# Tile 3's sums on VectorE and GpSimd placed anew, one preparation later, and another order of matmuls in the retention blocks

## The chip, the cores and the metric

One core of a Trainium2 chip. The time is that of the device for one execution of the whole program, in microseconds (us). TensorE (PE) multiplies matrices; its weight loads (PEld) run beside its matmuls. VectorE (DVE), ScalarE (ACT) and GpSimd (POOL) work elementwise, SyncE (SP) issues most of the transfers. Each engine runs its own instructions in order; semaphores hold an instruction back until another engine's result is there.

## The reference

A retention layer (attention with decay instead of a softmax) feeds a two-layer network whose activation is `h * cos(h)`:

```
B, H, S, D = 8, 8, 576, 64
ret = (q @ k.T) / sqrt(D) * Dmat     # Dmat[i, j] = gamma_h ** (i - j) if i >= j, else 0
x   = (ret @ v), heads side by side  # 4608 tokens x 512
h   = x @ w_in                       # 512 -> 2048
g   = h * cos(h)
out = g @ w_out                      # 2048 -> 512
```

All inputs and the output are float32; the kernel multiplies in bfloat16 and adds up in float32.

## The kernel before

The 4608 tokens are 36 groups of 128. The network takes them in ten tiles, of 512, 256 and 256 tokens and then seven of 512. Tile 3 is the first of these seven (in the code `S7 = 3`) and holds groups 8 to 11; tile 4 holds groups 12 to 15.

**Retention.** A group is loaded (`load`, three transfers for q, k and v on SyncE's queue into five buffers each), prepared on GpSimd (`prep`: q and k times powers of gamma, lines 139 and 140, and v cast to bfloat16, line 147), and transposed by a transfer on SyncE's queue (`transposes`, line 156). SyncE takes loads, transposes and stores in the order in which the code asks for them, and a transpose waits there until GpSimd has prepared its group. `scores` multiplies key by query on TensorE and masks the result to `ret` on VectorE (line 192). `states` keeps the running sum of key times value (TensorE line 242, VectorE lines 263 and 265; ScalarE copies it to `sb`, line 256). `attn_out` gives the group's result out of two kinds of matmul into one PSUM bank: state times query (line 283) and `ret` times v (line 296); ScalarE copies it to `xT`. From tile 3 on, `unit7` does this for two groups at a time: `states` for the next, `attn_out` for these two, and then the scores of the two after them. These are the retention blocks; PSUM bank "b" serves the states first and the second of the two scores afterwards.

**Network.** `mm1` makes `h` in eight blocks of a tile (line 323); ScalarE takes the cosine (line 331), VectorE multiplies both to `gT` (line 332). From tile 3 on the second matmul goes by Winograd's form of Strassen's method: the tile is cut into 2 x 2 quarters, and seven products of quarters replace eight. They run in the order 3, 4, 5, 2, 1, 7, 6 (`mm2_seven`, `product`, line 455). Products 3 and 4 read `gT` itself, the others a sum or difference of two quarters of `gT`, called X5, X2, X1, X7 and X6 here, in two halves of 128x1024 each (`g_sum`, line 401). `on_dve` there says which sums go to VectorE; all others go to GpSimd, and the first GpSimd sum after a VectorE sum is made to wait for it ("port free"). `sums_after` places the sums behind the blocks of `mm1`; tile 3 has placings of its own, there and in `more_sums`. In tile 3 these blocks go through the first half of the tokens (blocks 0 to 3) and then the second half (4 to 7); X5 needs the first half alone.

In tiles 3 and 4 the retention work stands inside the seven products like this: before product 5 only scores (`scores2`), before product 1 a retention block, before product 6 another, in tile 3 without scores. Tile 3 computes the scores of groups 12 to 15, tile 4 those of 16 to 21.

**What is prepared when.** Each store of a quarter of the output calls `feed`, which prepares groups up to a count that the code sets, then asks for their transposes and for further loads. Before tile 3, 16 groups (0 to 15) are prepared. During tile 3 the counts after its four stores are 17, 18, 19 and 22; in tile 4 they are 22, 23, 24 and 26. Group 16 is prepared by `more_sums`, so that the first of these calls finds it done. The order on each engine is the order of the code: nothing is scheduled anew.

Of the kernel before, what the change touches and what calls it, by code (L numbers as in the profile page):

```python
# [17 lines left out]
def kernel(  # L18
# [16 lines left out]
    nc = tc.nc  # L35
    P = 128
    B, H, S, D = q.shape
    assert (B, H, S, D) == (8, 8, 576, 64)
    HG = H // 2
# [4 lines left out]
    NG = NTOK // P  # L44
    PER = 2 * S // P
    MIX = PER // 2
    HP = P // 2
# [7 lines left out]
    starts = [sum(widths[:n]) for n in range(len(widths))]  # L55
    N_PE_T = 6
    S7 = 3
# [42 lines left out]
    tiles = {}  # L100
# [167 lines left out]

        return add

    def attn_out(gs, bank, evac=nc.vector.tensor_copy):


        ps = psum.tile([P, len(gs), HG, P], F32, tag=bank, name="ov")
        for x, g in enumerate(gs):
            c = g % PER
            if c == 0:
                continue
            qT = tiles["a", g][3]
            sb = tiles.pop(("sb", g))  # L280
            n = HP if c == MIX else P
            for hg in range(HG):
                nc.tensor.matmul(  # L283
                    ps[:, x, hg, :n],
                    lhsT=sb[:, hg, :],
                    rhs=qT[:, hg, :n],
                    start=(hg == 0),
                    stop=False,
                    skip_group_check=True,
                )  # L290
        for x, g in enumerate(gs):
            vb = tiles["a", g][1]
            ret = tiles.pop(("ret", g))
            for hg in range(HG):
                for he in range(2):
                    nc.tensor.matmul(  # L296
                        ps[he * D : he * D + D, x, hg, :],
                        lhsT=vb[:, 2 * hg + he, :],
                        rhs=ret[:, he, hg, :],
                        start=(g % PER == 0 and hg == 0),  # L300
                        stop=(hg == HG - 1),
                        skip_group_check=True,
                    )
        n = max(m for m in range(len(starts)) if starts[m] <= gs[0] * P)
        if ("x", n) not in tiles:
            tiles["x", n] = xp.tile([P, DG, 512], BF16, tag="xT", name="xT")
        t0 = gs[0] * P - starts[n]
        evac(  # L308
            tiles["x", n][:, :, t0 : t0 + len(gs) * P].rearrange("p c (x i) -> p x c i", i=P), ps
        )  # L310
# [43 lines left out]
    E2 = ET // 2  # L354
    N2 = DM // 2
    w_sum = {}
    last = len(widths) - 1
# [25 lines left out]
    def g_sum(n, x, e0, e1):  # L383

        gT = tiles["g", n]
        a, b, op_ = {
            5: ((0, 0), (0, 1), ALU.add),
            2: ((1, 0), (1, 1), ALU.add),
            1: ((0, 0), (1, 1), ALU.add),
            7: ((0, 1), (1, 1), ALU.subtract),  # L390
            6: ((1, 0), (0, 0), ALU.subtract),
        }[x]
        if ("gs", n, x) not in tiles:
            tiles["gs", n, x] = sump.tile([P, E2, 256], BF16, tag=f"gs{x}", name=f"gs{x}")
        i0, i1 = (
            gT[:, k * E2 + e0 : k * E2 + e1, r * 256 : (r + 1) * 256] for r, k in (a, b)
        )
        on_dve = x == 5 or (n, x) in ((S7, 1), (S7, 2)) or (n, x, e0) in (
            (last, 1, 0), (last, 2, 4), (S7 + 1, 2, 4)
        )  # L400
        i = (nc.vector if on_dve else nc.gpsimd).tensor_tensor(  # L401
            out=tiles["gs", n, x][:, e0:e1], in0=i0, in1=i1, op=op_
        )
        if on_dve:
            tiles["gate"] = i
        elif "gate" in tiles:
            tc.add_manual_dep(
                i.ins,
                tiles.pop("gate").ins.name,
                mybir.DependencyInfo(mybir.DependencyClass.Sync, mybir.DependencyReason.DATA),  # L410
                reason="port free",
            )

    def sums_after(n, i):

        if n == S7:
            if i < 4:
                w_sums(3 + i % 2, i // 2 * 4, i // 2 * 4 + 4)
            if i == 6:
                g_sum(n, 5, 0, 4)  # L420
            elif i == 7:
                g_sum(n, 5, 4, E2)
                g_sum(n, 2, 0, E2)
                g_sum(n, 7, 0, 4)
        elif i in (3, 7):
            for x in (5, 2, 1, 7, 6) if n < last or i > 3 else (5, 1, 2, 7, 6):
                g_sum(n, x, i - 3, i + 1)

    def product(n, x):
# [31 lines left out]
                skip_group_check=True,  # L461
            )
        return parts

    def more_sums(n):

        if n == S7:
            g_sum(n, 7, 4, E2)
            prep_next()
            g_sum(n, 1, 0, E2)  # L470
            for e in (0, 4):
                g_sum(n, 6, e, e + 4)

    def mm2_seven(n, at):

# [63 lines left out]
    def prep_next():  # L539
        nonlocal prepared  # L540
        prep(prepared)
        prepared += 1

    def feed(s):

        nonlocal loaded, prepared, transposed
        before = loaded
        n, r = divmod(s - starts[S7] // P, 4)
        if n >= 0:
            while prepared < min(NG, starts[S7] // P + 10 + 4 * n + ((0, 1, 2, 4) if n else (-1, 0, 1, 4))[r]):  # L550
                prep_next()
            while transposed < prepared:
                transposes(transposed)
                transposed += 1
            ahead = starts[S7] // P + 14 if n == 0 and r < 3 else prepared + LD
            while loaded < min(NG, prepared + LD, ahead):
                load(loaded)
                loaded += 1
            return
        while True:  # L560
            while prepared < min(loaded, 2 * s + 7, s + 11, starts[S7] // P + 8):
                prep(prepared)
                prepared += 1
                if transposed < N_PE_T:
                    transposed += 1

            if N_PE_T <= transposed < min(prepared, s + 11) and (
                transposed <= loaded - 2 or loaded == NG or (s > 3 and loaded == before)
            ):
                transposes(transposed)  # L570
                transposed += 1
            elif loaded < min(NG, 2 * s + 8, s + 13):
                load(loaded)
                loaded += 1
            else:
                break
# [58 lines left out]
    for h0, bank, evac in ((0, "b", nc.scalar.copy), (HG, "m", nc.vector.tensor_copy)):  # L635
# [8 lines left out]
        ps = psum.tile([P, 2, P, G4], F32, tag=bank, name="tr")  # L644
        for r in range(G4):
            for j in range(2):
                nc.tensor.matmul(
                    ps[:, j, :, r],
                    lhsT=qs4[:, r, h0 + 2 * j : h0 + 2 * j + 2, :].rearrange("p h d -> p (h d)"),
                    rhs=ident,  # L650
                    start=True,
                    stop=True,
# [42 lines left out]
    def scores2(g):  # L695
        if g < NG:
            scores(g, "a")
            scores(g + 1, "b")
# [12 lines left out]
    def unit7(g, more=True, then=lambda: None):  # L711

        copy = states([g + 1, g + 2], "b")()
        then()
        attn_out([g, g + 1], "m", nc.scalar.copy)
        if more:
            scores2(g + 2)
        copy(nc.scalar.copy)

    late = []  # L720
    for n, w in enumerate(widths):
# [8 lines left out]
        else:  # L730
            m = 1024 // w
# [17 lines left out]
        g = starts[n] // P + w // P  # L749
        if n == 0:  # L750
            todo = [
                (34 + 5 * i, lambda x=x, e=e: w_sums(x, e, e + 4))
                for i, (x, e) in enumerate((x, e) for x in (1, 6, 7) for e in (0, 4))
            ] + [
                (45, lambda: transposes(4, "ab")),
                (49, lambda: state(4)),
                (50, lambda: scores(4, "a")),
                (57, lambda: attn_out([4], "a")),
                (61, lambda: transposes(5, "ba")),
                (63, lambda: state(5)),  # L760
            ]
        elif n == 1:
            todo = pair(6, "ab", 16, 27)
        elif n == 2:
            todo = [(11, lambda: scores2(g)), (25, lambda: unit(g, "m", soon=True))]
            late += [lambda: unit(g + 2, "b", False)]
        else:
            at = {}
            if n + 1 < len(widths):
                at = {  # L770
                    5: lambda then: unit7(g, True, then),
                    1: lambda then: unit7(g + 2, True, then),
                }
                if n in (3, 4):
                    at = {
                        5: lambda then: (then(), scores2(g), more_sums(n)),
                        1: lambda then: unit7(g, True, then),
                        6: lambda then: unit7(g + 2, n > 3, then),
                    }
            mm2_seven(n, at)  # L780
            continue
        todo.sort(key=lambda u: u[0])
        order = [(tsi, et) for tsi in range(w // P) for et in range(ET)]
        if n == 0:

            part = 3 * ET // 4
# [38 lines left out]
```

## Time and profile before

| what | value |
|---|---|
| median of three runs | 302.14 us (302.12 to 302.67) |
| the profiled execution | 302.56 us, of which 300.9 us is its span |
| TensorE busy / idle in 94 to 124 us (tile 3 and the start of 4) | 27.74 / 2.26 us |
| TensorE busy / idle in 124 to 151 us (rest of tile 4) | 24.69 / 2.31 us |
| TensorE busy / idle in 151.2 to 181.4 us (tile 5) | 30.09 / 0.11 us |
| GpSimd busy in the same three | 25.71, 25.68, 25.00 us |

The granted TensorE clock is 1.00 throughout. "Idle" is the stretch less the busy time. Lines of the profile such as `98.80 0.60 POOL L147 CAST vb<-fv ... x1` give the start and the length in us, the engine, the line of the kernel, the operation, the tile written and those read, and how many instructions were merged; in brackets stands the idle time before and what ended it.

### The profile page before, as it was taken

What the parts mean: (1) busy time and instruction counts of PE and PEld (TensorE: products, weight loads), DVE (VectorE), ACT (ScalarE), POOL (GpSimd) and SP (SyncE); (2) the same over time, 40 slices, a digit from 0 to 9 for tenths busy, and PEclk for the clock granted to TensorE, in tenths of its full rate; (3) what the DMA queues carried; (4) which work ended last, traced back from release to release, by engine and by line L of the source; (5) the groups of instructions that cost most, each with busy time, mean ns of one, the idle gap of its engine ahead of it and who ended that gap; (6) DMA issues with size and microseconds to landing.
All of it is one profiled execution on the core that took longest, in us unless ns stands there. A gap on an engine that the chain in (4) does not pass through costs nothing.

```text
span 300.9 us, 6641 instructions
## 1 busy us (share of the span) xinstructions
PE 288.5 (96%) x2740; PEld 199.4 (66%) x2761; DVE 209.7 (70%) x250; ACT 145.7 (48%) x187; POOL 200.2 (67%) x165
## 2 busy tenths in 40 slices
PE   7899999999999979997999999999999999999995
PEld 3478647858588867465844885488448854884594
DVE  6777636664699994789858774877488748835872
ACT  3556333515255354651456574648465646524620
POOL 2770076445445499999975997599859925970583
PEclk9999999999999999999999999999999999999999
DMA  8999999999999999999999988994850250022013
GB/s 210 212 210 207 206 219 191 207 253 199 219 184 201 204 215 226 225 258 188 193 247 216 243 212 147 236 215 122 184 131 2 72 139 2 0 72 70 2 35 105
DMA packets 154269, 50.23 MB, mean 167 GB/s; under 512 B 140800, under 2 KB 153216, under 8 KB 154240
## 3 DMA queue, kind: packets, MB, share of 16 engines
q1 hardware_dynamic: 150016, 45.63, 75.1%
q0 software_dynamic: 4224, 4.19, 8.4%
q8 instruction: 21, 0.34, 0.5%
q14 instruction: 8, 0.07, 0.1%
HBM read 36.70 MB, written 9.44 MB: 153 GB/s over the span
## 4 chain that ended last, share of the span: by engine, by line
PE 51%; DVE 1%; issue 0%; DVEq 0%
PE h L323 23%; PE o L455 22%; PE ov L296 2%; PE sc L183 2%; PE ov L283 2%; PE st L242 1%; DVE ret L192 1%; DVE ot L484 0%; DVEq L820 0%
## 5 line engine op out<-in xcount | busy, mean ns | idle before, releaser
L401 POOL TENSOR_TENSOR gs<-gT 128x1024 bf16<-128x1024 bf16 x49 | 104.9, 2173 | 43.0 <-DVE gs L401 42.4
L323 PE MATMUL h<-xT,w_in_sb 128*128 128x512 bf16 (+2 forms) x820 | 127.1, 313 | 1.4 <-DVE gT L332 0.5
L332 DVE TENSOR_TENSOR gT<-h,cosh 128x1024 bf16<-128x1024 f32 x72 | 87.9, 1223 | 43.6 <-ACT cosh L331 43.4
L331 ACT ACTIVATE cosh<-h,half_pi 128x1024 f32<-128x1024 f32 x72 | 80.2, 1114 | 64.1 <-PE h L323 62.9
L323 PEld LDWEIGHTS <-w_in_sb 128*128 128x128 bf16 x832 | 75.8, 98 | 49.8 <-issue 1.1
L139 POOL TENSOR_TENSOR qks<-fq,gq 128x512 bf16<-128x512 f32 x32 | 35.5, 1109 | 38.7 <-DMA fq<-in_q_dram 36.7
L455 PEld LDWEIGHTS <-gs 128*128 128x128 bf16 x576 | 53.9, 98 | 9.4 <-issue 1.9
L140 POOL TENSOR_TENSOR qks<-fk,gk 128x512 bf16<-128x512 f32 x35 | 37.4, 1068 | 9.8 <-DMA fk<-in_k_dram 9.1
L192 DVE TENSOR_TENSOR ret<-sc,tri 128x1024 bf16<-128x1024 f32 x32 | 38.0, 1219 | 3.8 <-PE sc L183 3.7
L455 PE MATMUL o<-ws,gs 128*128 128x256 bf16 (+1 forms) x352 | 38.4, 268 | 0.0
L484 DVE TENSOR_TENSOR ot<-o,ot 128x512 f32<-128x512 f32 (+2 forms) x32 | 19.7, 620 | 14.7 <-PE o L455 14.6
L340 PE MATMUL o<-w_out_sb,gT 128*128 128x512 bf16 x121 | 28.8, 380 | 0.4 <-issue 0.2
L308 ACT CAST xT<-ov 128x1024 bf16<-128x1024 f32 (+1 forms) x18 | 16.5, 918 | 25.8 <-PE ov L296 25.6
L455 PE MATMUL o<-w_out_sb,gs 128*128 128x256 bf16 x224 | 25.8, 273 | 1.8 <-DVE ot L484 1.8
L455 PE MATMUL o<-w_out_sb,gT 128*128 128x256 bf16 x224 | 25.6, 273 | 0.0
L455 PEld LDWEIGHTS <-gT 128*128 128x128 bf16 x224 | 21.8, 98 | 3.9
L340 PEld LDWEIGHTS <-gT 128*128 128x128 bf16 x128 | 11.8, 98 | 12.6
L401 DVE TENSOR_TENSOR gs<-gT 128x1024 bf16<-128x1024 bf16 (+1 forms) x19 | 19.6, 1046 | 0.4
L256 ACT CAST sb<-s 64x256 bf16<-64x256 f32 x40 | 16.1, 403 | 0.9 <-DVE s L263 0.4
L147 POOL CAST vb<-fv 128x512 bf16<-128x512 f32 x22 | 13.9, 632 | 2.6 <-DMA fv<-in_v_dram 2.4
L350 ACT COPY ot<-o 128x512 f32<-128x512 f32 x8 | 4.7, 588 | 17.1 <-PE o L340 17.0
L484 DVE TENSOR_TENSOR ot<-ot,o 128x512 f32<-128x512 f32 x14 | 9.6, 682 | 4.7 <-ACT ot L509 2.7
(70 smaller groups left out, 174.2 us busy)
## 6 DMA issues: line engine op xcount, KB each, us to landing
out_dram<-ot SPq DMA_DIRECT2D x35, 256.0 KB, 3.4
fk<-in_k_dram SPq DMA_DIRECT2D x32, 256.0 KB, 4.9
fv<-in_v_dram SPq DMA_DIRECT2D x32, 256.0 KB, 5.1
fq<-in_q_dram SPq DMA_DIRECT2D x28, 256.0 KB, 4.6
w_in_sb<-in_moe_w_in_dram POOLq DMA_DIRECT2D x4, 512.0 KB, 9.0
w_out_sb<-in_moe_w_out_dram POOLq DMA_DIRECT2D x4, 512.0 KB, 16.2
fq<-in_q_dram SPq DMA_DIRECT2D x2, 512.0 KB, 4.4
fq<-in_q_dram SPq DMA_DIRECT2D x8, 128.0 KB, 4.0
```

The costliest lines, as they stand in the source:

```text
L139: nc.gpsimd.tensor_tensor(out=qks[:, 0], in0=fq, in1=tq, op=ALU.mult)
L140: (nc.vector if g == 3 else nc.gpsimd).tensor_tensor(out=qks[:, 1], in0=fk, in1=tk, op=ALU.mult)
L192: nc.vector.tensor_tensor(out=ret.rearrange("p a b i -> p (a b) i"), in0=ps.rearrange("p a b i -> p (a b) i"), in1=mask.unsqueeze(1).to_br ...
L256: run(sb[r, :, r], s[r])
L308: evac(tiles["x", n][:, :, t0 : t0 + len(gs) * P].rearrange("p c (x i) -> p x c i", i=P), ps)
L323: nc.tensor.matmul(ps[:, j, :], lhsT=w_in_sb[:, dg, (et + j) * P : (et + j + 1) * P], rhs=xT[:, dg, c0 : c0 + w], start=(dg == 0), stop=(d ...
L331: nc.scalar.activation(cosh, ps, ACTF.Sin, bias=half_pi, scale=1.0)
L332: nc.vector.tensor_mul(gT[:, et : et + m, c0 : c0 + w], ps, cosh)
L340: nc.tensor.matmul(ps, lhsT=gT[:, et, tsi * P : (tsi + 1) * P], rhs=w_out_sb[:, et, :], start=(et == 0), stop=(et == ET - 1),)
L401: i = (nc.vector if on_dve else nc.gpsimd).tensor_tensor(out=tiles["gs", n, x][:, e0:e1], in0=i0, in1=i1, op=op_)
L455: nc.tensor.matmul(dst[i], lhsT=lhs[:, e, j * P : (j + 1) * P], rhs=rhs[:, e, c0:c1], start=(x in (3, 4, 1, 7) and e == 0 and (i == 0 or l ...
L484: pend.append(lambda: nc.vector.tensor_tensor(out=out_, in0=in0, in1=in1, op=op_))
```

## The change

1. X5's two halves in tile 3 are computed behind blocks 4 and 5 of `mm1`, where they stood behind 6 and 7.
2. X1 in tile 3 goes to GpSimd in two halves (it was one VectorE sum of 128x2048); all of X1, X7 and X6 stand in one run behind block 7, and `more_sums` is gone.
3. Group 16 is prepared behind block 6, ahead of all these sums; before, X7's halves stood ahead of it.
4. Tile 3 prepares one group less: the count after its fourth store is 21. Group 21 is prepared at the first store of tile 4, which stands behind tile 4's eight GpSimd sums.
5. X2's second half in tile 4 goes to GpSimd.
6. `attn_out` in `unit7` runs all `ret` times v matmuls first and the state times query ones after them; the flags that open and close the PSUM accumulation move accordingly. Other calls of `attn_out` keep their order.

```diff
-    def attn_out(gs, bank, evac=nc.vector.tensor_copy):
+    def attn_out(gs, bank, evac=nc.vector.tensor_copy, own_first=False):
...
+        def carried():
...
                 for hg in range(HG):
                     nc.tensor.matmul(
                         ps[:, x, hg, :n],
                         lhsT=sb[:, hg, :],
                         rhs=qT[:, hg, :n],
-                        start=(hg == 0),
-                        stop=False,
+                        start=(not own_first and hg == 0),
+                        stop=(own_first and hg == HG - 1),
                         skip_group_check=True,
                     )
+        def own():
...
+                            start=((own_first or alone) and hg == 0),
+                            stop=((not own_first or alone) and hg == HG - 1),
...
+        for part in (own, carried) if own_first else (carried, own):
+            part()
...
-        on_dve = x == 5 or (n, x) in ((S7, 1), (S7, 2)) or (n, x, e0) in (
-            (last, 1, 0), (last, 2, 4), (S7 + 1, 2, 4)
-        )
+        on_dve = x == 5 or (n, x) == (S7, 2) or (n, x, e0) in ((last, 1, 0), (last, 2, 4))
...
         if n == S7:
             if i < 4:
                 w_sums(3 + i % 2, i // 2 * 4, i // 2 * 4 + 4)
-            if i == 6:
-                g_sum(n, 5, 0, 4)
-            elif i == 7:
-                g_sum(n, 5, 4, E2)
+            elif i < 6:
+                g_sum(n, 5, i % 4 * 4, i % 4 * 4 + 4)
+            elif i == 6:
+                prep_next()
+            else:
                 g_sum(n, 2, 0, E2)
-                g_sum(n, 7, 0, 4)
+                for x in (1, 7, 6):
+                    for e in (0, 4):
+                        g_sum(n, x, e, e + 4)
...
-    def more_sums(n):
-
-        if n == S7:
-            g_sum(n, 7, 4, E2)
-            prep_next()
-            g_sum(n, 1, 0, E2)
-            for e in (0, 4):
-                g_sum(n, 6, e, e + 4)
...
-            while prepared < min(NG, starts[S7] // P + 10 + 4 * n + ((0, 1, 2, 4) if n else (-1, 0, 1, 4))[r]):
+            while prepared < min(NG, starts[S7] // P + 10 + 4 * n + ((0, 1, 2, 4) if n else (-1, 0, 1, 3))[r]):
...
         copy = states([g + 1, g + 2], "b")()
         then()
-        attn_out([g, g + 1], "m", nc.scalar.copy)
+        attn_out([g, g + 1], "m", nc.scalar.copy, own_first=True)
...
-                        5: lambda then: (then(), scores2(g), more_sums(n)),
+                        5: lambda then: (then(), scores2(g)),
```

## The prediction, made before the changed kernel had run

> **What bounds the kernel now.** I read the page's totals first, then the chain that ended last, then TensorE's waits, and last the timelines of TensorE, VectorE, GpSimd and SyncE from 94 to 160 us, where tiles 3 and 4 run.
>
> ```profile
> span 300.9 us, 6641 instructions
> PE 288.5 (96%) x2740; PEld 199.4 (66%) x2761; DVE 209.7 (70%) x250; ACT 145.7 (48%) x187; POOL 200.2 (67%) x165
> PE 51%; DVE 1%; issue 0%; DVEq 0%
> ```
>
> TensorE is busy for 96% of the span and the end of the chain is nearly all TensorE. So only two things move the time: idle TensorE, and the TensorE work itself. The waits name the idle time, and all the large ones lie in tiles 3 and 4:
>
> ```profile
> PE o L455 <- DVE ot L484: 1.8, 1, 1.8
> PE sc L183 <- DVE s L265: 1.7, 1, 1.7
> PE h L323 <- DVE gT L332: 0.5, 1, 0.5
> PE st L242 <- DVE ret L192: 0.4, 1, 0.4
> ```
>
> From 151 us on TensorE has no idle time to win: 30.09 busy of 30.20 us in tile 5. But GpSimd is busy for 25.00 of the same 30.20, so it has 5 us to spare in a tile. What GpSimd (POOL) and SyncE (SP) do here:
>
> ```profile
> 98.80 0.60 POOL L147 CAST vb<-fv 128x512 bf16<-128x512 f32 x1
> 103.69 4.21 POOL L401 TENSOR_TENSOR gs<-gT 128x1024 bf16<-128x1024 bf16 x2 [4.29 <-DVE gs L401]
> 107.86 2.03 POOL L139 TENSOR_TENSOR qks<-fq,gq 128x512 bf16<-128x512 f32 x1
> ...
> 110.83 0.61 POOL L147 CAST vb<-fv 128x512 bf16<-128x512 f32 x1
> 111.41 4.21 POOL L401 TENSOR_TENSOR gs<-gT 128x1024 bf16<-128x1024 bf16 x2
> ```
> ```profile
> 98.88 1.23 SPq L156 DMA_TRANSPOSE qkT<-qks  x1
> 100.16 0.57 SPq L114 DMA_DIRECT2D fq<-in_q_dram  x1
> 100.79 0.62 SPq L114 DMA_DIRECT2D fk<-in_k_dram  x1
> 101.45 0.77 SPq L114 DMA_DIRECT2D fv<-in_v_dram  x1
> ```
> ```profile
> fv<-in_v_dram SPq DMA_DIRECT2D x1, 256.0 KB, 6.0
> ```
>
> The reader is to see three things. One sum of half a product's operand costs GpSimd 2.1 us (4.21 for two). The load of group 16, the next one to be prepared, is issued only at 100.16 to 101.45, behind the transpose of group 15. Its V part lands 6.0 us after its issue, at 107.45. GpSimd uses the group at 107.86, so today this lateness costs nothing.
>
> **What the Trainium skill says.** "SBUF — State Buffer", section "Who interferes with whom": a VectorE tensor_tensor with both inputs in SBUF shares a read port with GpSimd, and whichever starts first blocks the other for a whole instruction. The trace agrees: a VectorE weight sum that takes 0.69 us alone took 1.40 us at 94.98, when GpSimd was in a 1.04 us multiply, and GpSimd's cast behind it took 1.07 us in place of 0.61. "GPSIMD Engine Reference", section 2.1, has about 2.5 cycles an element as the floor of a two-input operation; the trace's 2.1 us for 1024 elements is what I use. "Perfetto Trace Analysis", section "DMA Instruction — HWDGE (DVE, Sync)": the recorded length of a DMA instruction leaves out the data's movement. It agrees: 0.77 us of issue against 6.0 us to landing above.
>
> **The change part by part.** Times are on the clock of the profile before.
>
> X5 earlier. Its two halves (0.68 us each) now stand on VectorE behind the gT multiplies of blocks 4 and 5, where they stood behind 6 and 7. Block 4's multiply ends at 97.52. GpSimd is then in a multiply until 97.85, so the first half runs to 98.5, block 5's multiply (1.22) to 99.7, the second half, behind GpSimd's cast, to 100.7, block 6's multiply to 101.9, block 7's to 103.1. Product 4 starts at 101.1 (1.8 us after product 3 at 99.31). It needs block 6's result at once and block 7's half a product later: it waits 0.8 and then 0.2 us. Cost +1.0. Without the port it would be 0.45, at most 1.1. In return X2's sum still ends at about 104.2, since VectorE's total work up to there is the same. The blocked GpSimd also brings group 15's transpose, and group 16's load behind it, 0.65 us later.
>
> X1 on GpSimd. VectorE loses the 2.59 us sum at 106.39. The state sums that free bank b then end at about 109.3, and the second scores want it at 109.5. The wait of 1.67 goes: -1.67.
>
> The preparation of group 16 ahead of the sums. In the built program its three GpSimd instructions now stand before all six remaining sums; before, two sums stood ahead of it. GpSimd runs in order, so the sums wait for group 16's V: 107.45 + 0.65 = 108.1, cast to 108.7. Then X1's halves end at 110.8 and 112.9, X7's at 115.0 and 117.1, X6's at 119.2 and 121.3. TensorE, 1.0 us late, is ready for product 1 at 110.1 (107.07 + 1.0, and 2.05 for the retention block). It waits for each half: the product's second half begins at 113.0, product 7's at 117.2, product 6's at 121.4, and tile 3 ends at 122.3 against 117.7. The two parts above are in this: net +4.6. What was hidden under two sums now stands alone.
>
> One group later. GpSimd prepares four groups, not five, after tile 3's sums: 4 x 2.56 = 10.3 us, to 131.6. Tile 4's sums wait for X5's first half (127.91 before, 132.5 now), then eight of them take 17.2 us as in tile 5 (one now is X2's second half): to 149.7. Only then, in program order, comes group 21, which before was ready at about 129. Its two multiplies end at 151.75. SyncE then issues the transpose; those in this stretch land 3.6 to 4.5 us after issue, I take 4.2: 155.95. But the last retention block of tile 4 computes the scores of groups 20 and 21. TensorE would be there at 117.7 + 4.6 plus 31.2 - 2.1 for the rest, 151.4 in all. So it waits about 4.5 us. Behind the waiting scores stand product 6 and tile 5's whole first product, and nothing can pass them. From the second scores to the tile's end is 2.25 us (148.93 to 151.18): tile 4 ends at 158.2, +7.0 in all.
>
> X2's second half off VectorE in tile 4 takes away 1.77, and the 0.36 after it, both hidden under the wait for group 21: nothing. It would be -2.13 if that wait were not there. On GpSimd it ends at 143.6, when product 2's second half wants it at 143.0: hidden too.
>
> Ret times v ahead. Same matmuls, other order, in twelve retention blocks. The weight loads pause where the tile shape changes (from 199.34 to 199.45 and from 199.93 to 200.02 in tile 6's first block). States and ret times v have one shape (128*64), so one change goes, and one not seen before comes. I take -0.05 a block, between 0 and -0.1; a loss is not excluded, but a block has one change less, so I leave it out. It counts in the eight blocks of tiles 5 to 8 alone: -0.4. The results it reads (ret, tiles of the block before) are long done, so there is no new wait.
>
> Later tiles. GpSimd comes out of tile 4 with five preparations to do (149.7 to some 163.3) and tile 5's sums cannot start before 168: its 5 us of slack cover this.
>
> Sum: +7.0 - 0.4 = +6.6. On the profiled execution (302.56, of which 300.9 is span) that makes 309.2. It lies 0.42 above the median of 302.14, so I put the forecast at 308.7.
>
> **Rivals.**
> A, the forecast: both waits. Its ends: V lands after 5.0 us with no port delay, the transpose after 3.6, the order wins 0.8: +4.0, 306.1; the other ends (port 1.1, landing 6.3, transpose 4.5, order nothing): +7.8, 309.9.
> B: only one wait decides. If group 16 landed before 104, tile 3 would end about 0.7 early, tile 4's sums run 127.9 to 145.1 and group 21's transpose land at 151.4: tile 4 ends at 153.6, +2.4. If instead only tile 3's wait is real, it is 4.6 - 2.1 = +2.5. With -0.4 both give 304.2. For it: landing times scatter from 3.6 to 6.3. Against: GpSimd's order is fixed, and eight sums and two multiplies are ahead of group 21 wherever they start.
> C, the other side: the change does what its edits aim at. It wins 1.67 + 1.77 + 0.36 + 0.4 and pays 1.0: -3.2, 298.9. Its one condition is a GpSimd queue that is never late: group 16 whole by 104 and group 21 transposed by 149. The 6.0 us landing speaks against it.
> D: the delayed loads behind group 21's transpose reach tile 5's scores too: +10, 312.1. Against: the 5 us of slack.
>
> **How the numbers follow.** A 0.74, B 0.15, C 0.07, D 0.04. The range of 304.0 to 310.2 holds A and B. Within 0.2% (0.6 us, what these runs can tell from no change) lies only a mixture of B and C: faster 0.06, same 0.02, slower 0.92.
>
> **What would show it.** TensorE waits for gT in product 4 (1 us), for GpSimd's sums in products 1, 7 and 6 of tile 3, and for the last transpose before the second scores at the end of tile 4; the waits of 1.67 and 1.77 are gone; GpSimd idles about 4 us for a DMA before group 16's cast. The prediction is wrong if group 16's V lands by 105, or if TensorE doesn't wait at the end of tile 4.

## The result and the profile after

The changed kernel takes 309.66 us (median of four runs, 309.12 to 310.41) against 302.13 for the kernel before: a ratio of 1.0248, with a 95% interval of 1.0222 to 1.0273. It is slower by 7.5 us; 308.7 had been forecast. The profile below is of the run of 310.41, whose span is 308.7 us, 7.8 more than before.

TensorE's waits in the changed kernel (engine, operation and line, what it waited for; total us, times, longest):

```profile
PE sc L183 <- DMA qkT<-qks: 5.8, 1, 5.8
PE o L463 <- POOL gs L406: 2.4, 3, 1.0
PE o L463 <- DVE ot L483: 1.0, 1, 1.0
PE o L463 <- DVE gT L339: 0.5, 1, 0.5
```

The waits of 1.7 us (scores for the state sums in tile 3) and 1.8 us (product 2 in tile 4) are gone. In their place stand one wait of 5.8 us for a transpose and several for sums on GpSimd. The wait put down to `ot` is one of these: TensorE's order has product 7's weights wait for GpSimd there, and X7's first half ends at that time. The TensorE timeline shows where they are:

```profile
101.28 2.18 PE L463 MATMUL o<-w_out_sb,gT 128*128 128x256 bf16 x16 [0.54 <-DVE gT L339]
...
112.39 1.05 PE L463 MATMUL o<-ws,gs 128*128 128x256 bf16 x8 [1.04 <-DVE ot L483]
114.46 1.05 PE L463 MATMUL o<-ws,gs 128*128 128x256 bf16 x8 [1.03 <-POOL gs L406]
...
118.63 1.05 PE L463 MATMUL o<-ws,gs 128*128 128x256 bf16 x8 [0.87 <-POOL gs L406]
119.51 13.98 PE L330 MATMUL h<-xT,w_in_sb 128*128 128x512 bf16 x64
...
148.30 0.40 PE L183 MATMUL sc<-qkT 64*128 64x128 bf16 x8
154.50 0.61 PE L183 MATMUL sc<-qkT 64*128 64x128 bf16 x8 [5.80 <-DMA qkT<-qks]
155.03 3.60 PE L463 MATMUL o<-ws,gs 128*128 128x256 bf16 x16
158.42 15.08 PE L330 MATMUL h<-xT,w_in_sb 128*128 128x512 bf16 x64
```

The last two lines are what the prediction had not reckoned with. Product 6, sixteen matmuls, took 1.92 us before and takes 3.60 here; tile 5's first product took 13.98 and takes 15.08. No wait is shown in them. The stretches of 2 us around them tell why (us, then busy time of TensorE, weight loads, VectorE, ScalarE, GpSimd; then the granted clock, the share of the DMA engines, which can pass 1 since transfers count in the stretch in which they start, and GB/s):

```profile
148.00:150.00 2.00, 0.69 (x14) 0.41 (x12) 1.85 (x3) 1.56 (x3) 2.00 (x3) 1.00 0.76 161
150.00:152.00 2.00, 0.00 (x0) 0.00 (x0) 0.00 (x0) 1.06 (x3) 2.00 (x3) 0.60 1.01 259
152.00:154.00 2.00, 0.00 (x0) 0.00 (x0) 0.00 (x0) 0.00 (x0) 1.86 (x4) 0.50 1.17 184
154.00:156.00 2.00, 1.50 (x13) 1.07 (x14) 0.85 (x1) 0.00 (x0) 2.00 (x3) 0.50 1.32 209
156.00:158.00 2.00, 2.00 (x12) 1.39 (x11) 0.37 (x1) 0.00 (x0) 2.00 (x4) 0.50 1.26 256
158.00:160.00 2.00, 2.00 (x7) 0.91 (x6) 0.69 (x1) 0.00 (x0) 2.00 (x3) 0.50 1.05 240
160.00:162.00 2.00, 2.00 (x9) 0.88 (x8) 0.00 (x0) 0.49 (x1) 0.55 (x1) 0.84 1.27 241
```

While TensorE idles, its granted clock falls to half, 1.7 us into the wait (at 150.40), and it stays there for some 6 us after the work has begun again (to 160.64). The wait of 5.8 us thus costs another 2.7: 1.6 in product 6 (3.39 from its start to the next product's, 1.76 before) and 1.1 in tile 5.

GpSimd and SyncE around the two places:

```profile
102.90 1.61 POOL L139 TENSOR_TENSOR qks<-fq,gq 128x512 bf16<-128x512 f32 x1 [4.08 <-DMA fq<-in_q_dram]
104.48 1.04 POOL L140 TENSOR_TENSOR qks<-fk,gk 128x512 bf16<-128x512 f32 x1
105.46 0.60 POOL L147 CAST vb<-fv 128x512 bf16<-128x512 f32 x1
106.03 12.54 POOL L406 TENSOR_TENSOR gs<-gT 128x1024 bf16<-128x1024 bf16 x6
...
129.79 17.16 POOL L406 TENSOR_TENSOR gs<-gT 128x1024 bf16<-128x1024 bf16 x8 [0.99 <-DVE gs L406]
146.92 1.04 POOL L139 TENSOR_TENSOR qks<-fq,gq 128x512 bf16<-128x512 f32 x1
147.92 1.04 POOL L140 TENSOR_TENSOR qks<-fk,gk 128x512 bf16<-128x512 f32 x1
```
```profile
147.81 1.15 SPq L114 DMA_DIRECT2D fv<-in_v_dram  x1
149.06 1.02 SPq L490 DMA_DIRECT2D out_dram<-ot  x1
150.19 1.32 SPq L156 DMA_TRANSPOSE qkT<-qks  x1
```

Group 16's cast starts at 105.46, straight behind its multiply, so its V was there by then. Group 21's q and k are ready at 148.96, its transpose is issued at 150.19, behind group 25's load and a store, and lands 4.3 us later.

The profiled executions differ by up to 5 us before tile 3 begins, so the experiments are compared by stages as well: from the start of a stage on TensorE to the start of the next.

| us | product 3 of tile 3 starts | tile 3's products | tile 4 | tile 5 | rest |
|---|---|---|---|---|---|
| before | 99.31 | 18.39 | 33.32 | 30.23 | 119.65 |
| changed | 98.83 | 20.68 | 38.91 | 31.12 | 119.16 |
| e1 order alone | 104.28 | 18.17 | 33.12 | 30.03 | 119.20 |
| e2 group 21 early | 100.04 | 20.67 | 33.70 | 30.02 | 119.17 |
| e3 group 16 late | 99.06 | 24.57 | 36.34 | 30.17 | 119.16 |
| e4 wait filled | 102.31 | 20.04 | 36.72 | 30.03 | 119.16 |
| e5 changed again | 99.30 | 20.67 | 35.64 | 30.96 | 119.13 |
| e6 as e4 | 99.16 | 21.41 | 36.73 | 30.03 | 119.17 |
| e7 group 21 late alone | 99.12 | 18.39 | 40.60 | 30.65 | 119.64 |
| e8 X2 on GpSimd alone | 99.35 | 20.07 | 31.64 | 30.24 | 119.60 |
| e9 as e7, shorter queue | 99.19 | 18.40 | 35.21 | 30.24 | 119.56 |
| e10 wait half filled | 99.38 | 21.83 | 38.94 | 30.02 | 119.17 |
| e11 X1 behind the states | 99.42 | 20.02 | 31.88 | 30.02 | 119.16 |
| e12 as e11, X2 behind X5 | 102.88 | 20.04 | 30.84 | 30.02 | 119.12 |

The change's +7.8 us is the sum of its row against the first: -0.5 + 2.3 + 5.6 + 0.9 - 0.5. On the chips of the experiments single runs of most kernels, the one before too, come out 2 to 8 us longer than the others, the profiled ones of e1, e10 and e12 among them; the medians are over all runs, and the ratios leave out those more than 1.5% above the fastest of their kernel.

### The profile page after: what moved, and what is told of

The parts are those of the page before. It is cut to its first block, busy times and chain, and to the rows that moved or that the text cites. A ratio compares the mean times of both kernels' runs of the same rounds, so it can differ in the third digit from the quotient of the medians.

```text
span 308.7 us, 6666 instructions
## 1 busy us (share of the span) xinstructions
PE 292.9 (95%) x2761; PEld 199.8 (65%) x2761; DVE 203.7 (66%) x248; ACT 145.5 (47%) x187; POOL 205.9 (67%) x168
## 4 chain that ended last, share of the span: by engine, by line
PE 67%; POOL 12%; DMA 9%; SPq 6%; issue 3%; DVE 0%; ACT 0%; DVEq 0%; POOLq 0%
PE h L330 31%; PE o L463 21%; PE o L347 6%; POOL gs L406 6%; SPq L114 5%; DMA fq<-in_q_dram 4%; POOL qks L140 3%; POOL qks L139 2%; PE sc L183 2%; PE ov L300 2%; PE ov L284 2%; DMA fk<-in_k_dram 2%; POOL vb L147 2%; DMA qkT<-qks 1%; DMA fv<-in_v_dram 1%
## 5 line engine op out<-in xcount | busy, mean ns | idle before, releaser
L406 POOL TENSOR_TENSOR gs<-gT 128x1024 bf16<-128x1024 bf16 x52 | 111.0, 2172 | 42.6 <-DVE gs L406 42.6
L330 PE MATMUL h<-xT,w_in_sb 128*128 128x512 bf16 (+2 forms) x832 | 128.8, 315 | 0.2
L463 PE MATMUL o<-ws,gs 128*128 128x256 bf16 (+1 forms) x352 | 40.6, 275 | 2.9 <-POOL gs L406 1.9
L347 PE MATMUL o<-w_out_sb,gT 128*128 128x512 bf16 x128 | 30.1, 380 | 0.0
L183 PE MATMUL sc<-qkT 64*128 64x128 bf16 x256 | 10.7, 220 | 5.8 <-DMA qkT<-qks 5.8
L183 PEld LDWEIGHTS <-qkT 64*128 64x128 bf16 x288 | 8.4, 95 | 11.2 <-DMA qkT<-qks 6.0
L406 DVE TENSOR_TENSOR gs<-gT 128x1024 bf16<-128x1024 bf16 (+1 forms) x17 | 13.9, 825 | 0.4
```

What stands on the lines that cost most here:

```text
L183: nc.tensor.matmul(ps[:, he, hg, :], lhsT=qkT[d0 : d0 + D, HG + hg, :], rhs=qT[d0 : d0 + D, hg, :], start=True, stop=True,)
L330: nc.tensor.matmul(ps[:, j, :], lhsT=w_in_sb[:, dg, (et + j) * P : (et + j + 1) * P], rhs=xT[:, dg, c0 : c0 + w], start=(dg == 0), stop=(d ...
L347: nc.tensor.matmul(ps, lhsT=gT[:, et, tsi * P : (tsi + 1) * P], rhs=w_out_sb[:, et, :], start=(et == 0), stop=(et == ET - 1),)
L406: i = (nc.vector if on_dve else nc.gpsimd).tensor_tensor(out=tiles["gs", n, x][:, e0:e1], in0=i0, in1=i1, op=op_)
L463: nc.tensor.matmul(dst[i], lhsT=lhs[:, e, j * P : (j + 1) * P], rhs=rhs[:, e, c0:c1], start=(x in (3, 4, 1, 7) and e == 0 and (i == 0 or l ...
```

## The experiments

**e1 to e4, one chip.** The kernel before took 302.52 there.

e1 puts the new order of the retention blocks into the kernel before (the new `attn_out` of the change comes with it):

```diff
-        attn_out([g, g + 1], "m", nc.scalar.copy)
+        attn_out([g, g + 1], "m", nc.scalar.copy, own_first=True)
```

> The kernel before with the new order in the retention blocks alone. Theory (one change of tile shape less in twelve blocks; tiles 6 to 9 of the changed kernel were 0.5 us shorter than before): 0.4 to 0.9 us faster, 301.2 to 301.7. Rival (those 0.5 us are chance, the order is worth nothing): 302.1, within 0.2 us of the kernel before. Other sign possible (the new change of shape costs more): 302.4 or above.

301.86, ratio 0.9946 (0.9896 to 0.9997), 0.7 below the kernel before by the medians, as the theory has it. The stages are clearer than the total: tiles 3, 4 and 5 are each 0.20 to 0.22 us shorter than before, the rest 0.45. Every kernel with the new order has 30.02 to 30.03 in a tile 5 without half clock and 119.12 to 119.20 in the rest; those with the old one (before, e7, e8, e9) have 119.56 to 119.65. With two blocks in a tile and six in the rest, the gain is about 0.1 us a block. The weight loads show where it comes from. First a whole second retention block of tile 6 before, then of the changed kernel:

```profile
204.17 0.33 PEld L242 LDWEIGHTS <-qks 128*64 128x64 bf16 x16 [0.21 <-issue]
204.54 0.22 PEld L283 LDWEIGHTS <-sb 128*128 128x128 bf16 x4
204.87 0.48 PEld L296 LDWEIGHTS <-vb 128*64 128x64 bf16 x16
205.44 0.47 PEld L183 LDWEIGHTS <-qkT 64*128 64x128 bf16 x16
```
```profile
212.34 0.33 PEld L242 LDWEIGHTS <-qks 128*64 128x64 bf16 x16 [0.21 <-issue]
212.59 0.48 PEld L300 LDWEIGHTS <-vb 128*64 128x64 bf16 x16
213.16 0.23 PEld L284 LDWEIGHTS <-sb 128*128 128x128 bf16 x4
213.49 0.59 PEld L183 LDWEIGHTS <-qkT 64*128 64x128 bf16 x16
```

From the first load of the states to the first of the scores it is 1.27 before and 1.15 after. The gain lies where ret times v (64 columns) now follows the states (64 columns too): 0.25 us after their start instead of 0.37 for the step from the states to the 128 columns of `sb`.

e2 is the changed kernel with group 21 prepared in tile 3 again, e3 the changed kernel with group 16 prepared behind the six sums:

```diff
# e2, in feed
-            ... else (-1, 0, 1, 3))[r]):
+            ... else (-1, 0, 1, 4))[r]):
# e3, in sums_after
-            elif i == 6:
-                prep_next()
-            else:
+            elif i == 7:
                 g_sum(n, 2, 0, E2)
...
                         g_sum(n, x, e, e + 4)
+                prep_next()
```

> The changed kernel with group 21 prepared in tile 3 again (count 22). Theory L (group 21's lateness sets the end of tile 4): the wait of 5.8 us and the slow clock behind it (some 2.8 us) go, tile 4's sums come 1.6 us later and product 2 waits 2.1 us in place of 0.5; 302.7, between 302 and 303.5. Rival P (what costs is the load on GpSimd in tiles 3 and 4 as a whole, and the wait only moves to the sums): above 306.

306.81, ratio 1.011 (1.0056 to 1.0164); its profiled execution took 305.29. By the median the rival's range is met, by the profiled execution neither. The stages of that execution say what happened: the wait for group 21 and the half clock are gone, and tiles 4 and 5 together take 63.72 us against 70.03, 6.3 less where 7.0 were expected. The 5.8 us wait and its 2.7 us of half clock are therefore group 21's. The medians show less: 4.3 us above the kernel before, where the changed kernel had 7.5. The three runs that were not profiled took 1.2 to 1.9 us more than this one, and why isn't known. In the stages the missing part is a new wait. VectorE's half of X5 in tile 4 now falls among the preparations and stands there for 2.87 us:

```profile
130.22 2.87 DVE L406 TENSOR_TENSOR gs<-gT 128x1024 bf16<-128x1024 bf16 x1
```

TensorE waits 1.32 us for the gT multiply behind it. What keeps this execution slower than before is tile 3, 20.67 against 18.39.

> The changed kernel with group 16 prepared behind tile 3's six sums instead of ahead of them. Theory L: the 2.9 us of waits for sums in tile 3 go, but the scores of group 21 still come at 154 to 155, so the wait there grows by as much: 309.2 to 310.2, no change. Rival T (the waits of tile 3 and tile 4 add up): 2.9 us faster, 306.8.

312.46, ratio 1.0308 (1.0239 to 1.0377): a miss for both theories, and my oversight. The waits for sums in tile 3 do go, but another takes their place:

```profile
PE st L242 <- POOL vb L147: 5.4, 1, 5.4
```

The last retention block of tile 3 builds the states of groups 15 and 16, and so wants group 16's v. Group 16 can't be prepared behind the sums; that is why it has to stand in the middle of them in the kernel before. This edit tells nothing about whether tile 3's and tile 4's waits add up.

e4 keeps TensorE at work during the wait with matmuls whose result is overwritten:

```diff
-            scores(g + 1, "b")
+            scores(g + 1, "b", idle=24 if g == 20 else 0)
```

> The changed kernel with 24 idle matmuls of 512 columns (24 x 0.213 = 5.1 us) on TensorE before the scores of group 21, so that TensorE works through the wait; their result is overwritten. Theory C (TensorE's granted clock falls to half in the 5.8 us of idling and comes back only 6 us after): the clock stays at 1.00, product 6 takes 1.8 us and not 3.6, the first product of tile 5 13.8 and not 14.9: 2.5 to 2.9 us faster, 306.8 to 307.2. Rival D (the slowness behind the wait is from transfers or from weights coming late): unchanged, 309.7.

309.13, ratio 1.0203 (1.015 to 1.0255). The mechanism shows in the trace, the gain hardly in the total: product 6 takes 1.92 us and tile 5's first product 13.98, both as before the change, at a clock of 1.00 throughout. But this profile began tile 3 3.5 us late for reasons ahead of the change, so it was repeated.

**e5 to e8, another chip** (before: 302.71). e5 is the changed kernel itself, e6 is e4's kernel.

> The changed kernel once more, as the measure for the next one on the same chip. Expected: 7.0 to 7.8 us above the kernel before; a wait of 5 to 6.5 us before the scores of group 21, and a granted clock of 0.5 from about 3 us into that wait to some 6 us behind it.

> The changed kernel with the 24 idle matmuls again, now beside e5 on one chip. Theory C (half clock behind the wait): 2.3 to 2.9 us below e5. Rival D (the first time's total, 309.1, was right and the clock costs less than 1 us): within 1 us of e5.

e5 took 309.19 (1.0209, 1.0152 to 1.0267), e6 308.41 (1.0172, 1.0119 to 1.0226): 0.8 us apart, so by the totals the rival is right. e5 itself missed what was expected of it: it lies 6.5 us above the kernel before, and its wait is shorter. The two profiles give the reason. In e5 the transpose is issued at 149.45 and lands 3.3 us later, the wait is 3.63 us, and the clock falls only 1.3 us after the work has begun again (at 154.08): product 6 lasts 2.71, tile 5's first product 14.91. In e6 the issue comes at 150.66 and the filling lasts 5.3 us whatever the wait would have been. Filling removes the 1.7 us that half clock costs in e5 and gives them back: tiles 4 and 5 together take 66.60 us in e5 and 66.76 in e6. That the half clock follows the wait is shown, since it is gone in both profiles with the wait filled; the saving of 2.3 to 2.9 us is not.

e7 is the kernel before with one digit changed, e8 with one pair taken out:

```diff
# e7, in feed
-            ... else (-1, 0, 1, 4))[r]):
+            ... else (-1, 0, 1, 3))[r]):
# e8, in g_sum
-            (last, 1, 0), (last, 2, 4), (S7 + 1, 2, 4)
+            (last, 1, 0), (last, 2, 4)
```

> The kernel before with group 21 prepared in tile 4 (count 21) and nothing else. GpSimd then has one preparation less ahead of tile 4's sums and would have group 21's q and k at about 145.7. Theory Q (SyncE's queue: the transpose stands behind four groups' loads and a store, which it gets through at 149 to 150): landing at 153.5 to 154.5, a wait of about 5 us, the half clock behind it: 309 to 310. Rival G (GpSimd alone decides): landing at 149.8, a wait of 1 us: 303.1.

309.77, ratio 1.0221 (1.0172 to 1.0271). Preparing group 21 later is enough for the whole loss. Theory Q holds. GpSimd has the group's q and k ready at 145.54, and SyncE issues the transpose at 149.46, behind the load of group 25 and a store; it lands 4.7 us later:

```profile
143.50 1.04 POOL L139 TENSOR_TENSOR qks<-fq,gq 128x512 bf16<-128x512 f32 x1
144.50 1.04 POOL L140 TENSOR_TENSOR qks<-fk,gk 128x512 bf16<-128x512 f32 x1
```
```profile
147.28 1.01 SPq L114 DMA_DIRECT2D fv<-in_v_dram  x1
148.38 0.97 SPq L491 DMA_DIRECT2D out_dram<-ot  x1
149.46 1.37 SPq L156 DMA_TRANSPOSE qkT<-qks  x1
```
```profile
154.18 0.61 PE L183 MATMUL sc<-qkT 64*128 64x128 bf16 x8 [6.91 <-DMA qkT<-qks]
154.72 3.60 PE L455 MATMUL o<-ws,gs 128*128 128x256 bf16 x16
```

TensorE resumes at 154.18, against 154.50 in the changed kernel, though tile 3 cost nothing here. This answers what e3 left open: the edits to tile 3 make tile 4 begin later, and the wait for group 21 swallows most of that.

> The kernel before with the second half of X2 in tile 4 on GpSimd and nothing else. Theory: behind four first halves from 129.3 it ends at 140.5 when product 2 wants it at 137.5: 3.0 us of wait in place of 1.77, the 0.36 goes: 303.0, 0.5 to 1.2 us slower. Rival (the edit does what it aims at): both waits go, 300.0.

302.73, ratio 1.0007 (0.9979 to 1.0035): neither the theory nor the rival. In the profile tile 4 is 1.68 us shorter, only 0.50 of its waits being left, and tile 3, which this edit doesn't touch, is 1.68 longer: after the old wait of 1.67 us the clock fell to half, and products 1 and 7 took 5.33 us in place of 3.67. A tile 4 that begins that late meets its sums in time. What the edit is worth without this stays open.

**e9 to e12, a third chip** (before: 302.63). e9 is e7 with one group less ahead of the transpose on SyncE's queue:

```diff
-            ahead = ... else prepared + LD
+            ahead = ... else prepared + LD - (n == 0)
```

> e7 (the kernel before with group 21 late) with one group less loaded ahead of group 21's transpose on SyncE's queue (group 25's load comes behind the transpose). Theory Q (the queue holds the transpose back from 145.5 to 149.5): issue at 145.5 to 146, landing at 149.7, a wait of about 2.4 us in place of 6.9, and the clock mostly holds: 302.5 to 304.5. Rival G (the late preparation on GpSimd decides): as e7, 309 to 310.

305.40, ratio 1.0073 (1.0043 to 1.0103), and 304.32 in the profiled execution. The preparation is as late as in e7, but the transpose goes out at 145.66, 3.8 us earlier, lands after 3.4 us in place of 4.7, and the wait shrinks from 6.91 to 1.75 us:

```profile
149.10 0.41 PE L183 MATMUL sc<-qkT 64*128 64x128 bf16 x8 [1.75 <-DMA qkT<-qks]
149.44 3.53 PE L455 MATMUL o<-ws,gs 128*128 128x256 bf16 x16
```

By the ratios (1.0221 and 1.0073) two thirds of e7's loss were the queue, not GpSimd. The total lies above what was expected, at least in part since the clock did not hold: product 6 takes 3.53 us even behind this short wait.

e10 is e4 with `idle=12`:

> The changed kernel with 12 idle matmuls (12 x 0.22 = 2.6 us) at the start of the wait for group 21, short enough to end inside it every time. Theory C: the rest of the wait is too short to bring the clock down, product 6 takes 1.75 to 1.9 us and tile 5's first product 13.8; 1.8 to 2.8 us below the changed kernel's 309.2 to 309.7: 306.9 to 307.9. Rival: the clock falls all the same, no gain.

307.91, ratio 1.0128 (1.0044 to 1.0212). The gain about fits in size, but the profiled execution, the longest of the four at 311.06, doesn't show the reason given: behind the filling TensorE still waited 3.14 us, the clock fell all the same, and product 6 took 3.36. The three others, of 305.97 to 308.30 us, have mean granted clocks of 0.994 to 0.998, the changed kernel's runs 0.981 to 0.994, so the clock may well have held there. Whether the theory fits them isn't shown; e9's wait of 1.75 us shows that a short rest need not leave the clock alone.

e11 and e12 look for a version better than both. e11 is e1 with X1's VectorE sum in tile 3 moved behind the state sums; e12 adds a new place for X6's first half in tile 4:

```diff
# e11, on top of e1
             prep_next()
-            g_sum(n, 1, 0, E2)
             for e in (0, 4):
                 g_sum(n, 6, e, e + 4)
...
+    def late_sum(n):
+
+        if n == S7:
+            g_sum(n, 1, 0, E2)
...
-                        1: lambda then: unit7(g, True, then),
+                        1: lambda then: unit7(g, True, lambda: (then(), late_sum(n))),
# e12, on top of e11, in sums_after
+        elif n == S7 + 1 and i in (3, 7):
+            for x, e in {
+                3: ((5, 0), (2, 0), (1, 0), (7, 0)),
+                7: ((5, 4), (2, 4), (6, 0), (1, 4), (7, 4), (6, 4)),
+            }[i]:
+                g_sum(n, x, e, e + 4)
```

> A version meant to be better than both: the kernel before with the new order in the retention blocks, and X1's sum in tile 3 still on VectorE, but behind the state sums that free bank b instead of ahead of them. Expected: the wait of 1.67 shrinks to a wait for X1 of 0 to 1.3 us before product 1; with the 0.4 to 0.9 of the order 300.2 to 301.4. Rival (the sum waits for GpSimd's port as long as before, 2.6 us in all): no gain over e1, 301.5.

302.12, ratio 0.9983 (0.9953 to 1.0013): the rival. The wait only moves from the scores to product 1, and here the clock falls behind it too:

```profile
111.15 5.33 PE L462 MATMUL o<-ws,gs 128*128 128x256 bf16 x32 [2.06 <-DVE gs L408]
```

> e11, and in tile 4 X6's first half on GpSimd placed behind X2's second half on VectorE, so that VectorE's two sums there follow each other with one GpSimd sum between at most. Expected: the 1.77 before product 2's second half shrinks to 0 to 0.8 and the 0.36 behind it goes: 298.8 to 300.2. Rival (both sums still wait for a whole GpSimd sum each): as e11.

301.02, ratio 0.9943 (0.9912 to 0.9974): less than was expected, but 1.6 us below the kernel before and 1.1 below e11 by the medians, and the best of all kernels here (fastest run 299.63). Tile 4 takes 30.84 us against 33.32. Its two VectorE sums follow each other, 1.31 us for both where they took 4.57:

```profile
139.34 1.31 DVE L408 TENSOR_TENSOR gs<-gT 128x1024 bf16<-128x1024 bf16 x2
```

Of tile 4's old waits none is left, and 0.26 us before the scores of group 21 is the only one in that tile.

## Why the prediction was right, and by what

**X5 earlier (+1.0).** Right. Products 3 and 4 take 4.56 us to the scores behind them (98.83 to 103.39) in place of 3.61. The first half of X5 stood behind GpSimd's multiply and took 1.40 us; the second, forecast to stand behind the cast, took 0.68. The loss of 0.95 us is as forecast all the same.

**X1 on GpSimd (-1.67).** Right, the wait is gone. But GpSimd pays for it with two more sums, which the forecast books under the next point. Begun at 106.03 without them, X6 would have been done at some 114.4 (an estimate: four sums of 2.1 us), and it was done at 115.62 in the kernel before. So the waits below are X1's doing as much as group 16's.

**Group 16 ahead of the sums (tile 3 at +4.6).** The mechanism is right, its size was wrong by a factor of two: tile 3's products take 2.3 us more. That is the 0.95 of X5 and 2.94 of waits for sums, less the 1.67; no experiment took these apart. The term that was mis-sized is the landing of group 16's V. It was carried over as 6.0 us after an issue at 102.1. The issue came at 100.42, the landing after 4.8 us, at 105.2, and V was no longer what held GpSimd up: it waited 4.08 us for the group's q, and V was there when the two multiplies were done. So the sums started at 106.03 and not at 108.7, product 1 did not wait at all, and the waits of products 7 and 6 (1.04, 1.03, 0.87) are together about half of what the forecast had. A single landing time from one execution was used as if it were fixed; the loads of V alone scatter from 4.4 to 6.5 us in the two profiles. The mark set for "wrong", V landed by 105, was missed by 0.2 us.

**One group later (sum +7.0, tile 4's end at 158.2).** The wait is where it was put, 5.8 us against 4.5, and tile 4 ends at 158.42. But part of the agreement is luck. TensorE reached the wait 2.7 us earlier than forecast and left it 1.5 us earlier (154.5 against 155.95), since GpSimd's sums began 2.7 us earlier. What made this good is a term that the prediction didn't have: product 6 at half clock, 1.6 us, and 1.1 more in tile 5. "TensorE: Matmul & The Clock Gate", section "Part 1: The HAM clock gate", in the Trainium skill says that the clock is halved after an idle window of about 3.4 us and needs about as much work to come back; I had not applied it to my own forecast of a wait longer than that. The trace agrees that it is halved, but already 1.7 us into the wait, and has it back only some 6 us after work began.

The split of the sum was off too: the forecast had 4.6 us in tile 3 and 2.4 in tile 4, and the stages show 2.3, 5.6 and 0.9 more in tile 5. And e7 loses as much as the changed kernel by group 21 alone. That is rival B's mechanism, one wait that decides, at a size of 7 us that neither B (+2.4) nor the forecast had for it.

The forecast gave GpSimd's order the whole blame for group 21. In the changed kernel that is nearly so: q and k are ready at 148.96 and the queue adds 1.2 us, and in e5 it adds nothing (ready at 149.42, issued at 149.45). What the forecast didn't have is that SyncE's queue is late by itself: in e7 and e9 GpSimd is ready at 145.5 or so, and the queue alone makes the difference between a wait of 6.91 and one of 1.75 us. In e7 GpSimd is 3.4 us earlier than in the changed kernel, and the loss is the same.

**X2's second half on GpSimd.** Right in the changed kernel: product 2 waits 0.51 us for it, hidden under the wait behind it.

**Ret times v ahead (-0.4).** Right in sign and in mechanism; it is about 0.1 us a block and not 0.05, 0.65 us in tiles 5 to 8.

**Later tiles.** Right: GpSimd is idle again before tile 5's sums, and no tile after it waits.

Rival C failed on its one condition: group 16 was not whole by 104, and group 21 was transposed at 154.5 and not by 149. Of rival D nothing is seen: no wait follows in tile 5.

## What to carry to other kernels

A step moved later is as late as the slowest queue that it passes: look at the transfer queue as well as at the engine, and at who waits for the result at the far end; in e7 one digit in a table of counts cost 7 us, about two thirds of it because a transpose stood behind a group of loads that could have come after it (e9).

An idle stretch on a busy TensorE can have a second price, the half clock behind it. Here waits from about 1.7 us on could bring it about, and the one of 1.67 us in e8 cost another 1.66, so such a wait is priced with it.

Before work is given to an engine with idle time, count what it must do between its input and the first user: in the changed kernel six sums of 2.1 us start at 106.03, and TensorE without its waits for them would have wanted the last at some 115.7 (an estimate: 118.63 less the three waits), however idle the engine is on average. In e3, started at 103.92, none was waited for (product 6 came late there for another reason).

## What the runs showed of the hardware that had not been expected

**Short waits can halve the clock, and it depends on where they fall.** "TensorE: Matmul & The Clock Gate", section "Part 1: The HAM clock gate", in the Trainium skill has an idle window of about 3.4 us. In e8, e9, e11 and e12 waits of 1.67, 1.75, 2.06 and 2.07 us were followed by work at half clock (5.33 us in place of 3.67 for two products, 3.53 in place of 1.92 for one); in the profiles of the kernel before, of e7 and of e9 a wait of the same 1.67 us as in e8, in the same place, was not. The measurement decides, and the traces go some way to say why. The half clock comes in whole stretches of 3.41 us: it lasted one of them in e5, e8, e9, e11 and e12, two in e7 (6.83 us) and three in the changed kernel (150.40 to 160.64). Where the borders lie differs from one execution to the next. The stretches around the wait of 1.67 us, first in e8, then in the kernel before (columns as for the stretches of 2 us in the section on the result):

```profile
107.83:111.24 3.41, 1.74 (x40) 1.31 (x38) 3.38 (x6) 2.16 (x4) 3.41 (x4) 1.00 1.11 254
111.24:114.65 3.41, 3.41 (x19) 2.42 (x17) 2.44 (x3) 0.46 (x2) 3.41 (x3) 0.50 1.12 261
```
```profile
106.96:110.37 3.41, 1.89 (x50) 1.43 (x48) 3.38 (x5) 1.96 (x3) 3.41 (x3) 1.00 0.98 224
110.37:113.79 3.42, 3.27 (x35) 2.89 (x36) 3.42 (x5) 1.25 (x4) 3.42 (x4) 1.00 1.25 249
```

In e8 the wait lies in one stretch; in the kernel before a border (110.37) cuts it, and neither part of it is enough. The same reading for other waits:

| execution | stretch | TensorE busy in it, us | clock in the next stretch |
|---|---|---|---|
| e12, wait of 2.07 | 111.70 to 115.12 | 1.35 | 0.50 |
| e9, wait of 1.75 | 145.94 to 149.36 | 1.67 | 0.50 |
| changed, first part of the wait of 5.80 | 146.99 to 150.40 | 1.71 | 0.50 |
| e7, wait of 1.67 | 107.73 to 111.15 | 1.75 | 1.00 |
| e5, first part of the wait of 3.63 | 147.25 to 150.67 | 1.91 | 1.00 |
| e5, the rest of it | 150.67 to 154.08 | 1.29 | 0.50 |

In all the profiles here, from 8 us on, half clock followed every stretch at full clock with up to 1.6 us of TensorE work and none with 1.8 or more, about half of 3.41 us; in between both occur (e8's 1.74 was followed by it, e7's 1.75 not), so a wait of 1.67 us is at the edge. The way back takes more: in the changed kernel the stretch from 153.81 with 2.73 us of work left the clock at half, and only the full one from 157.23 ended it; in e1 one with 2.86 did. This rule is read off these executions; no run varied the length of a wait or its place to test it.

**A VectorE sum can stand for several GpSimd instructions in a row.** "SBUF — State Buffer", section "Who interferes with whom", in the Trainium skill has the one that starts first block the other for a whole instruction. In e2 VectorE's half sum began at 130.22 and ended at 133.09; between 129.95 and 132.55 GpSimd ran two multiplies and a cast back to back, and the sum, 0.69 us when undisturbed, ended 0.54 us after them. That the port is the reason is argued from the page; the trace shows only the times. The three GpSimd lines:

```profile
129.95 1.04 POOL L139 TENSOR_TENSOR qks<-fq,gq 128x512 bf16<-128x512 f32 x1
130.95 1.04 POOL L140 TENSOR_TENSOR qks<-fk,gk 128x512 bf16<-128x512 f32 x1
131.94 0.61 POOL L147 CAST vb<-fv 128x512 bf16<-128x512 f32 x1
```

In the changed kernel and in the kernel before such a sum waited for one GpSimd instruction only (1.40 us for 0.69). Why it was more here wasn't tried.
